# A global-filter and low-rank mixer kernel: stage-3 stores, group order and load lead rearranged

## The chip, the cores and the metric

The kernel runs on one core of a Trainium2 chip. The metric is the device time of one execution in microseconds (us). The profile is of one execution and has a span of 652.9 us.

## The reference

```python
def _attn_ref(x, filt_r, filt_i):            # x: 8 x 3136 x 256
    X = np.fft.rfft(x, axis=1)
    F = (filt_r + 1j * filt_i)[None, :, :]   # 1569 x 256
    return np.fft.irfft(X * F, n=x.shape[1], axis=1)

def _moe_ref(x, U, V, w_ch1, w_ch2):
    h = x.transpose(0, 2, 1) @ U @ V         # rank 32
    u = x + h.transpose(0, 2, 1)
    return u + np.maximum(u @ w_ch1, 0.0) @ w_ch2
```

The second function is applied to the result of the first. All inputs and outputs are float32; the kernel works in float16 with float32 accumulation.

## The kernel before

A sequence of 3136 positions is read as 64 x 49, and the Fourier transform over it is done as matmuls with small constant matrices. The eight batches are worked on in five units: two of one batch, then three of two batches (`UNITS`, L20). Each unit passes through four stages.

*Stage 1* (`f1`, L260) transforms the 64-long axis. It loads x on the GpSimd queue with a cast to f16, multiplies by `wf1` (L275 for unit 0, L284 for the others), copies the result from PSUM to the tile `asb` and stores it to the scratch tensor `ct1` in DRAM. In unit 0 the copies alternate between DVE (L279) and ACT (L277), and the stores between the sync queue and ACT's queue (L298). The position r=48 is a small separate piece (`al`, L313).

*Stages 2 and 3* (`mid`, L329) run over 33 frequencies k1 in the order of `KORDER`. For each, the tile `a2` read back from `ct1` (L324) is multiplied by `tf2` (L371, L376), DVE multiplies the result by the filter `fab` into `uv` (L379, L386), and two matmuls with `g3` (L342) give the inverse transform of that k1. ACT copies it into `esb` (L352), and it is stored to the scratch tensor `ct2`, two k1 at a time (L357), with single stores for the slots 0 and 31 (L354). The pool has three `esb` buffers of two k1 each. Unit 0 stores on the sync queue and the other units on the GpSimd queue. The second half of `fab` is a copy of the first with its two parts exchanged; only units 1 to 4 read it, and two SBUF-to-SBUF transfers make it (`mirror_filters`, L187 and L188).

*Stage 4 and the mixer* work on groups of tokens (`Group`, L434). `load_e2` (L406) reads `ct2` back as `e2` tiles and a small tile `e2l` for r=48. `low_rank` (L419) multiplies by the transformed U into `h1`. `stage4` (L443) makes the last transform and adds the V part, giving the mixer's input `ut`. `mm1` (L479) does one of eight chunks of 128 hidden channels with ReLU on ACT, and `mm2_part` (L502) does the second product of the previous group, adds the residual through an identity matmul (L499), copies to `och` (L537) and stores to the output (L492). A group has 512 tokens, except one per unit for r=48 with 64 tokens per batch, which comes last in its unit.

The order of the work is written out by hand (L541 to L613). Unit 0 passes through stages 1 to 3 alone. Then a loop over all groups with eight steps each runs `mm1` of the current group, `mm2_part` of the one before and, at t == 2, `stage4` of the next. A list `plan` says at which step a piece of stage 1 (`deal_f1`) or one k1 of stages 2 and 3 (`deal`) of a later unit goes in. The last pieces of `mid` end some steps before the unit's first group; `load_e2` follows at the step `mid_end`, and `low_rank` at nine steps ahead of the unit's first group. A step of the r=48 group counts as a full step here, although it has 64 or 128 columns instead of 512. The tile framework assigns buffers and semaphores and settles the instruction order of each engine from this program.

A tiny DVE copy into a tile (`hold`, L161) delays the transfer into that tile until its source has landed. In this way the loads of unit 0 are spread: `second_loads` (filters from the second part on, the rest of `tf2` and `g3`) wait for the first `a2`, `third_loads` (U, V, w1, w2) for a product in the middle of stage 2, and `fourth_loads` (x of unit 1) for `e2l`.

Of the kernel before, what the change touches and what calls it, by code (L numbers as in the profile page):

```python
# [102 lines left out]
def kernel(  # L103
# [92 lines left out]
    w2sb = cst.tile([128, 8 * DM], F16)  # L196

    def second_loads(src):
        for i in range(1, 4):
            hold(fab[0:1, 0, PARTS[i], 0:1], src)  # L200
            load_filters(PARTS[i], PARTS[i + 1])
        ka = PARTS[1] * 147
        hold(tf2[0:1, ka:ka + 1], src)
        nc.sync.dma_start(tf2[:, ka:], tf2_d[:, ka:])
        hold(g3[0:1, 2 * KA:2 * KA + 1], src)
        nc.sync.dma_start(g3[:, 2 * KA:], g_d[:, 2 * KA:])

    def third_loads(src):
        hold(usb[0:1, 0:1], src)
        nc.gpsimd.dma_start(usb, moe_U.rearrange("(q r) p -> q (r p)", q=NQ))  # L210
        nc.gpsimd.dma_start(vnat[0:32, :], moe_V)
        nc.gpsimd.dma_start(w1sb, moe_w_ch1.rearrange("(h dd) c -> dd h c", h=2))
        nc.gpsimd.dma_start(w2sb, moe_w_ch2.rearrange("(t cc) e -> cc t e", t=8))
# [46 lines left out]
    def f1(u, load_ahead=2):  # L260
# [4 lines left out]
        for c in range(nx):  # L265
# [47 lines left out]
        nc.scalar.copy(al, pf[0:m, 0, 0:DM])  # L313
# [16 lines left out]
    def mid(u, tag="z"):  # L330
# [4 lines left out]
        eng = nc.sync if u.n == 0 else nc.gpsimd  # L335

        def do_i1(k, uv):
# [14 lines left out]
            nc.scalar.copy(st["esb"][:, i, :], pe[0:98, 0:bd])  # L352
# [42 lines left out]
        while uvs:  # L395
            do_i1(*uvs.pop(0))
# [44 lines left out]
    groups = [Group(u, g) for u in units for g in range(u.ng + 1)]  # L441
# [37 lines left out]
    def mm1(gr, t):  # L479
        n = gr.ntok  # L480
        ph = ps.tile([128, 512], F32, tag="m", bufs=2, name="phh")
        for dh in range(2):
            nc.tensor.matmul(ph[:, 0:n], w1sb[:, dh * 1024 + t * 128:dh * 1024 + (t + 1) * 128],  # L483
                             gr.ut[:, dh, 0:n], start=(dh == 0), stop=(dh == 1))
# [58 lines left out]
    first = [sum(v.ng + 1 for v in units[:u.n]) * 8 for u in units]  # L543
# [22 lines left out]
    plan = [[] for _ in range(8 * len(groups) + 8)]  # L566

    def deal(gen, count, a, z):
        for i in range(count):
            assert a < z  # L570
            plan[a + i * (z - a) // count].append(gen)

    def deal_f1(u, a, at):

        k = a
        for _ in range(6 * u.nb + 1):
            while k % 8 not in at:
# [4 lines left out]
    for i in range(7):  # L582
        plan[(4, 5, 6, 7, 8, 9, 11)[i]].append(f1s[1])
    mid_end = [0, 42] + [first[u.n] - (21 if u.n == 2 else 25) for u in units[2:]]
    deal(mids[1], 34, 15, 41)
    deal_f1(units[2], 12, (0, 4, 6, 7))
    deal(mids[2], 34, 44, first[2] - 22)
    for u in units[3:]:
        deal_f1(u, first[u.n - 1] - 36, (4, 7))
        deal(mids[u.n], 34, first[u.n - 1] + 24, first[u.n] - 26)  # L590

    for n, gr in enumerate(groups):
        u = gr.u
        for t in range(8):
            mm1(gr, t)
            if t == 2 and n + 1 < len(groups):
# [3 lines left out]
            step = 8 * n + t  # L600
            for gen in plan[step]:
                next(gen)
            for v in units[2:]:
                if plan[step + 5].count(f1s[v.n]) and not v.x:
                    load_x(v, 0)
                    load_x(v, 1)
            if u.n + 1 < n_units:
# [36 lines left out]
```

## Time and profile before

| | |
|---|---|
| median of 3 runs | 656.44 us (655.64 to 658.65) |
| span of the profile | 652.9 us |
| PE busy | 573.9 us, 88% |
| DVE, ACT, POOL busy | 320.3, 334.2, 132.1 us |
| mean granted PE clock | 0.937 |
| DMA moved | 98.29 MB, mean 151 GB/s |
| first `mm1` matmul | 82.3 us |

Busy shares over the whole span mix a start-up in which units 0 and 1 are fed from DRAM, and a long part in which the mixer's matmuls run densely. The table by stretch, the chain of waits and the list of who waited for whom are therefore read for each stretch by itself. A unit boundary is where the first group of a new unit follows the last of the one before; these lie near 185, 275, 412 and 544 us.

### The profile page before, as it was taken

How to read it: one execution, taken by the hardware profiler on the slowest of the kernel's cores; microseconds unless marked ns; L12 is line 12 of the kernel's file. 1: busy time of each engine (PE TensorE's matmuls, PEld its weight loads, DVE VectorE, ACT ScalarE, POOL GpSimd, SP SyncE). 2: the span in 40 equal slices, each digit the busy share in tenths (PEclk: the TensorE clock that was granted, in tenths of full speed). 3: DMA queues.
4: the chain of work that ended last, by engine and by line, in shares of the span. 5: the costliest groups of instructions: out<-in, count | busy, mean ns of one | idle time of the engine just before them, and what ended most of it. 6: DMA issues, size and time to landing. Idle time of an engine off the chain costs nothing.

```text
span 652.9 us, 10703 instructions
## 1 busy us (share of the span) xinstructions
PE 573.9 (88%) x4161; PEld 383.9 (59%) x4161; DVE 320.3 (49%) x369; ACT 334.2 (51%) x625; POOL 132.1 (20%) x204
## 2 busy tenths in 40 slices
PE   3459249989879999699999999899999998999995
PEld 0347125656635666457666666576666775777774
DVE  2346114676567764135777752347777523333331
ACT  2213026655436666165666655555656654555553
POOL 4220604365431242030111231011111100000000
PEclk9955579998889999789999999999999999999999
DMA  9896687897994289964635289545261493033033
GB/s 170 228 213 143 141 168 154 194 223 194 203 307 122 75 183 237 282 115 104 178 97 166 48 221 283 143 111 163 85 190 41 124 210 104 3 98 82 16 98 104
DMA packets 44289, 98.29 MB, mean 151 GB/s; under 512 B 8194, under 2 KB 19104, under 8 KB 44042
## 3 DMA queue, kind: packets, MB, share of 16 engines
q1 hardware_dynamic: 25470, 57.98, 31.9%
q0 software_dynamic: 16800, 38.45, 27.3%
q10 hardware_dynamic: 1968, 1.17, 0.6%
q8 instruction: 32, 0.52, 0.3%
q14 instruction: 19, 0.16, 0.1%
HBM read 59.88 MB, written 51.38 MB: 170 GB/s over the span
## 4 chain that ended last, share of the span: by engine, by line
PE 62%; DMA 20%; issue 7%; POOL 4%; ACT 3%; SPq 3%; DVE 1%; ACTq 0%; POOLq 0%; DVEq 0%
PE phh L483 20%; PE pc L527 19%; PE pe L342 7%; DMA x<-in_x_dram 5%; PE pz L371 4%; DMA ct_0<-esb 3%; PE pu L468 3%; PE pc L499 3%; PE pu L474 3%; DMA e_2517<-ct_2 2%; DMA ct_1<-esb 2%; SPq L411 2%; PE pf L284 2%; DMA e_4187<-ct_3 1%; DMA ct_0<-asb 1%
## 5 line engine op out<-in xcount | busy, mean ns | idle before, releaser
L483 PE MATMUL phh<-ut,w1sb 128*128 128x512 f16 (+2 forms) x848 | 245.9, 370 | 3.9 <-DVE ut L477 2.6
L386 DVE TENSOR_TENSOR uv<-pz,fab 98x1024 f16<-98x1024 f32 (+1 forms) x132 | 141.8, 1087 | 53.8 <-PE pz L371 53.5
L352 ACT CAST esb<-pe 98x512 f16<-98x512 f32 (+1 forms) x160 | 79.5, 501 | 108.5 <-PE pe L342 69.0
L537 DVE COPY och<-pc 128x512 f32<-128x512 f32 x96 | 66.3, 690 | 104.8 <-PE pc L499 101.1
L483 PEld LDWEIGHTS <-w1sb 128*128 128x128 f16 x848 | 79.4, 100 | 43.8 <-issue 12.8
L477 DVE CAST ut<-pu 128x1024 f16<-128x1024 f32 x48 | 58.8, 1224 | 82.4 <-PE pu L474 82.1
L342 PE MATMUL pe<-uv,g_80 98*98 98x512 f16 (+1 forms) x330 | 91.3, 365 | 4.6 <-ACT esb L352 4.5
L342 PEld LDWEIGHTS <-g_80 98*98 98x98 f16 x330 | 45.6, 140 | 23.7 <-issue 10.9
L499 PE MATMUL pc<-idn,ut 128*128 128x128 f16 (+1 forms) x394 | 55.6, 222 | 0.0
L499 PEld LDWEIGHTS <-ut 128*128 128x128 f16 (+1 forms) x394 | 38.7, 99 | 6.5 <-issue 1.4
L284 PE MATMUL pf<-x,wf_64 128*128 128x512 f16 x84 | 27.0, 395 | 14.0 <-DMA x<-in_x_dram 11.2
L289 DVE CAST asb<-pf 128x1024 f16<-128x1024 f32 x21 | 25.7, 1223 | 25.7 <-PE pf L284 21.2
L156 POOL DMA_DIRECT2D x<-in_x_dram x48 | 26.2, 560 | 55.3 <-PE pf L284 25.2
L371 PEld LDWEIGHTS <-tf_77 98*98 98x98 f16 x165 | 23.0, 139 | 19.5 <-issue 16.3
L379 DVE TENSOR_TENSOR uv<-pz,fab 98x512 f16<-98x512 f32 x33 | 22.6, 691 | 15.6 <-PE pz L376 11.4
L357 POOL DMA_DIRECT2D ct_4<-esb x15 | 10.7, 712 | 72.2 <-ACT esb L352 65.8
L357 POOL DMA_DIRECT2D ct_3<-esb x15 | 10.7, 716 | 69.2 <-ACT esb L352 69.2
L287 ACT CAST asb<-pf 128x1024 f16<-128x1024 f32 x21 | 21.3, 1012 | 6.5 <-PE pf L284 4.8
L357 POOL DMA_DIRECT2D ct_2<-esb x15 | 11.0, 736 | 49.9 <-ACT esb L352 40.6
L284 PEld LDWEIGHTS <-wf_64 128*128 128x128 f16 x84 | 8.1, 100 | 21.5 <-DMA x<-in_x_dram 12.2
L424 PEld LDWEIGHTS <-ut_96 128*32 128x32 f16 x120 | 3.2, 101 | 24.7 <-DMA e_553<-ct_0 8.7
L357 POOL DMA_DIRECT2D ct_1<-esb x15 | 11.2, 746 | 20.8 <-ACT esb L352 20.7
(1483 smaller groups left out, 1152.5 us busy)
## 6 DMA issues: line engine op xcount, KB each, us to landing
out_dram<-och SPq DMA_DIRECT2D x96, 192.0 KB
x<-in_x_dram POOLq DMA_DIRECT2D x48, 256.0 KB, 7.8
out_dram<-och SPq DMA_DIRECT2D x16, 384.0 KB
ct_2<-asb POOLq DMA_DIRECT2D x12, 256.0 KB, 6.6
ct_3<-asb POOLq DMA_DIRECT2D x12, 256.0 KB, 5.9
ct_4<-asb POOLq DMA_DIRECT2D x12, 256.0 KB, 5.7
ct_2<-esb POOLq DMA_DIRECT2D x15, 196.0 KB, 4.1
ct_3<-esb POOLq DMA_DIRECT2D x15, 196.0 KB, 3.2
```

Source lines behind the costliest of these rows:

```text
L156: nc.gpsimd.dma_start(t[64 * p:64 * p + 64], dram(x.tensor, (u.b[0] * SEQ + 8 * c) * DM + st * p, [[NR * DM, 64], [1, 8 * DM]]))
L284: nc.tensor.matmul(pf[:, i, :], wf1, u.x[c][:, r:r + 2, :], start=True, stop=True)
L342: nc.tensor.matmul(pe[0:98, 0:bd], g3[:, (2 * k + l) * 98:(2 * k + l + 1) * 98], uv[:, l * bd:(l + 1) * bd], start=(k != 32 and l == 0), s ...
L352: nc.scalar.copy(st["esb"][:, i, :], pe[0:98, 0:bd])
L357: eng.dma_start(dram(u.ct2, (slot - 1) * 98 * bd, [[bd, 98], [98 * bd, 2], [1, bd]]), st["esb"])
L371: nc.tensor.matmul(pz[0:98, 0:bd], wz, a2[c][:, i, :], start=True, stop=True)
L386: nc.vector.tensor_mul(uv.rearrange("p (f b d) -> p f b d", f=2, b=nb), zin, fin)
L477: nc.vector.tensor_copy(gr.ut, pu)
L483: nc.tensor.matmul(ph[:, 0:n], w1sb[:, dh * 1024 + t * 128:dh * 1024 + (t + 1) * 128], gr.ut[:, dh, 0:n], start=(dh == 0), stop=(dh == 1))
L499: nc.tensor.matmul(o[:, dh * 128:dh * 128 + 128], gr.ut[:, dh, t0:t0 + n], idn, start=False, stop=(dh == 1), skip_group_check=True)
L527: nc.tensor.matmul(o, gr.h[tt][:, i * 128:(i + 1) * 128], w2sb[:, tt * DM:(tt + 1) * DM], start=(tt == 0), stop=False, skip_group_check=True)
L537: nc.vector.tensor_copy(dst, gr.pc.rearrange("p (b j d) -> p b j d", b=u.nb, j=u.jc))
```

## The change

- Stage-3 stores (`do_i1`): for one-batch units, four k1 go into one `esb` buffer and one store; for two-batch units still two. All units store on the sync queue. The last full k1 of the order and the k1 pair 0 and 32 keep stores of their own.
- Group order: the r=48 group of every unit but the last moves from the end of the unit to the place behind its third group.
- Lead: times in `plan` are counted in full steps (the r=48 group counts by its columns); stages 2 and 3 of units 1 and 2 end earlier, and `load_e2` and `low_rank` follow at steps counted from the unit's start. `stage4` moves from t == 2 to t == 4.
- Start-up: unit 0's stage-1 copies all go to DVE, the second filter part is loaded when stage 1 ends, x of unit 1 is requested as soon as the second `e2` tile has landed, and the mirror copies wait for `h1`.
- w2 is loaded with 8 KB contiguous for each partition instead of eight rows of 1 KB; the hidden channels are numbered accordingly, and `mm1` takes its 128 columns of w1 with a step of eight elements.
- The name of the change speaks of filler matmuls: neither version issues any.

```diff
+    w1v = w1sb.rearrange("p (h cc t) -> p h cc t", h=2, t=8)
+    def load_part(i, src):
+        hold(fab[0:1, 0, PARTS[i], 0:1], src)
+        load_filters(PARTS[i], PARTS[i + 1])
     def second_loads(src):
-        for i in range(1, 4):
-            hold(fab[0:1, 0, PARTS[i], 0:1], src)
-            load_filters(PARTS[i], PARTS[i + 1])
+        for i in range(2, 4):
+            load_part(i, src)
...
-        nc.gpsimd.dma_start(w2sb, moe_w_ch2.rearrange("(t cc) e -> cc t e", t=8))
+        nc.gpsimd.dma_start(w2sb, moe_w_ch2.rearrange("(cc t) e -> cc (t e)", t=8))
...
-                        if i:
-                            nc.scalar.copy(dst[:, i, :], pf)
-                        else:
-                            nc.vector.tensor_copy(dst[:, i, :], pf)
+                        nc.vector.tensor_copy(dst[:, i, :], pf)
...
-        nc.scalar.copy(al, pf[0:m, 0, 0:DM])
+        if u.n == 0:
+            nc.vector.tensor_copy(al, pf[0:m, 0, 0:DM])
+            load_part(1, al[0:1, 0:1])
+        else:
+            nc.scalar.copy(al, pf[0:m, 0, 0:DM])
...
-        eng = nc.sync if u.n == 0 else nc.gpsimd
+        ne = 4 // nb
...
-            slot = 0 if k == 32 else k
-            if slot % 2 == 1:
-                st["esb"] = sb.tile([98, 2, bd], F16, tag="esb", bufs=3, name="esb")
-            i = 1 - slot % 2
+            pos = 31 if k == 32 else k - 1
+            i = pos % ne
+            if i == 0:
+                st["esb"] = sb.tile([98, ne, bd], F16, tag="esb", bufs=3, name="esb")
             nc.scalar.copy(st["esb"][:, i, :], pe[0:98, 0:bd])
-            if slot in (0, 31):
-                eng.dma_start(dram(u.ct2, slot * 98 * bd, [[bd, 98], [1, bd]]),
-                                    st["esb"][:, i, :])
-            elif i:
-                eng.dma_start(
-                    dram(u.ct2, (slot - 1) * 98 * bd, [[bd, 98], [98 * bd, 2], [1, bd]]),
+            if pos in (30, 31):
+                nc.sync.dma_start(
+                    dram(u.ct2, (0 if pos == 31 else 31 - i) * 98 * bd,
+                         [[bd, 98], [98 * bd, 1 if pos == 31 else i + 1], [1, bd]]),
+                    st["esb"][:, i if pos == 31 else 0:i + 1, :])
+            elif i == ne - 1:
+                nc.sync.dma_start(
+                    dram(u.ct2, (k - i) * 98 * bd, [[bd, 98], [98 * bd, ne], [1, bd]]),
                     st["esb"])
...
-    groups = [Group(u, g) for u in units for g in range(u.ng + 1)]
+    groups = []
+    for u in units:
+        g = list(range(u.ng))
+        g.insert(3 if u.n + 1 < len(units) else u.ng, u.ng)
+        groups += [Group(u, i) for i in g]
...
-            nc.tensor.matmul(ph[:, 0:n], w1sb[:, dh * 1024 + t * 128:dh * 1024 + (t + 1) * 128],
+            nc.tensor.matmul(ph[:, 0:n], w1v[:, dh, :, t],
                              gr.ut[:, dh, 0:n], start=(dh == 0), stop=(dh == 1))
...
-    first = [sum(v.ng + 1 for v in units[:u.n]) * 8 for u in units]
+    when, starts = [], []
+    now = 0.0
+    for n, gr in enumerate(groups):
+        if n == 0 or gr.u is not groups[n - 1].u:
+            starts.append(now)
+        for _ in range(8):
+            when.append(now)
+            now += gr.ntok / 512
+    def step_at(w):
+        return next(i for i, v in enumerate(when) if v >= w)
...
     load_e2(units[0])
-    hold(fab[0:1, 1, 0, 0:1], units[0].e2l[0:1, 0:1])
-    hold(fab[64:65, 1, 0, 0:1], units[0].e2l[0:1, 0:1])
+    fourth_loads(units[0].e2[1][0:1, 0, 0, 0:1])
+    low_rank(units[0])
+    hold(fab[0:1, 1, 0, 0:1], units[0].h1[0:1, 0:1])
+    hold(fab[64:65, 1, 0, 0:1], units[0].h1[64:65, 0:1])
     mirror_filters(0, NK)
-    fourth_loads(units[0].e2l[0:1, 0:1])
-    low_rank(units[0])
     stage4(groups[0])
...
-    for i in range(7):
-        plan[(4, 5, 6, 7, 8, 9, 11)[i]].append(f1s[1])
-    mid_end = [0, 42] + [first[u.n] - (21 if u.n == 2 else 25) for u in units[2:]]
-    deal(mids[1], 34, 15, 41)
-    deal_f1(units[2], 12, (0, 4, 6, 7))
-    deal(mids[2], 34, 44, first[2] - 22)
+    deal(f1s[1], 7, 4, 11)
+    deal(mids[1], 34, 17, 34)
+    deal_f1(units[2], 12, (0, 2, 6, 7))
+    deal(mids[2], 34, 44, S[2] - 25)
+    load_step = {step_at(35): units[1], step_at(S[2] - 24): units[2]}
     for u in units[3:]:
-        deal_f1(u, first[u.n - 1] - 36, (4, 7))
-        deal(mids[u.n], 34, first[u.n - 1] + 24, first[u.n] - 26)
+        deal_f1(u, S[u.n - 1] - (38 if u.n == 3 else 48), (1, 7))
+        deal(mids[u.n], 34, S[u.n - 1] + (21 if u.n == 3 else 12), S[u.n] - 26)
+        load_step[step_at(S[u.n] - 25)] = u
+    rank_step = {step_at(S[u.n] - 6): u for u in units[1:]}
...
-            if t == 2 and n + 1 < len(groups):
+            step = 8 * n + t
+            if step in rank_step:
+                low_rank(rank_step[step])
+            if t == 4 and n + 1 < len(groups):
                 stage4(groups[n + 1])
...
-                if step == mid_end[u.n + 1]:
-                    load_e2(units[u.n + 1])
-                if step == first[u.n + 1] - 9:
-                    low_rank(units[u.n + 1])
+            if step in load_step:
+                load_e2(load_step[step])
```

`S[n]` is the start of unit n in full steps: 0, 49, 98, 196 and 294.

More of the change, by code (lines that the diff above doesn't have):

```diff
@@ L395, in mid @@
         while uvs:
-            do_i1(*uvs.pop(0))
+            last = uvs.pop(0)
+            do_i1(*last)
         yield
@@ L557 @@
     load_e2(units[0])
-    hold(fab[0:1, 1, 0, 0:1], units[0].e2l[0:1, 0:1])
-    hold(fab[64:65, 1, 0, 0:1], units[0].e2l[0:1, 0:1])
+    fourth_loads(units[0].e2[1][0:1, 0, 0, 0:1])
+    low_rank(units[0])
+    hold(fab[0:1, 1, 0, 0:1], units[0].h1[0:1, 0:1])
+    hold(fab[64:65, 1, 0, 0:1], units[0].h1[64:65, 0:1])
     mirror_filters(0, NK)
-    fourth_loads(units[0].e2l[0:1, 0:1])
-    low_rank(units[0])
     stage4(groups[0])
     plan = [[] for _ in range(8 * len(groups) + 8)]
+    S = starts
     def deal(gen, count, a, z):
         for i in range(count):
-            assert a < z
-            plan[a + i * (z - a) // count].append(gen)
+            plan[step_at(a + i * (z - a) / count)].append(gen)
     def deal_f1(u, a, at):
-        k = a
+        k = step_at(a)
         for _ in range(6 * u.nb + 1):
-            while k % 8 not in at:
+            while k % 8 not in at or groups[k // 8].last:
                 k += 1
@@ L580, in deal_f1 @@
             k += 1
-    for i in range(7):
-        plan[(4, 5, 6, 7, 8, 9, 11)[i]].append(f1s[1])
-    mid_end = [0, 42] + [first[u.n] - (21 if u.n == 2 else 25) for u in units[2:]]
-    deal(mids[1], 34, 15, 41)
-    deal_f1(units[2], 12, (0, 4, 6, 7))
-    deal(mids[2], 34, 44, first[2] - 22)
-    for u in units[3:]:
-        deal_f1(u, first[u.n - 1] - 36, (4, 7))
-        deal(mids[u.n], 34, first[u.n - 1] + 24, first[u.n] - 26)
+    deal(f1s[1], 7, 4, 11)
[3 more added lines that the diff above has]
+    load_step = {step_at(35): units[1], step_at(S[2] - 24): units[2]}
+    for u in units[3:]:
+        deal_f1(u, S[u.n - 1] - (38 if u.n == 3 else 48), (1, 7))
+        deal(mids[u.n], 34, S[u.n - 1] + (21 if u.n == 3 else 12), S[u.n] - 26)
+        load_step[step_at(S[u.n] - 25)] = u
+    rank_step = {step_at(S[u.n] - 6): u for u in units[1:]}
+    x_step = {max(0, next(i for i, p in enumerate(plan) if f1s[u.n] in p) - 5): u for u in units[2:]}
     for n, gr in enumerate(groups):
@@ L599 @@
                 mm2_part(groups[n - 1], t)
-            step = 8 * n + t
             for gen in plan[step]:
                 next(gen)
[L603 to L607, printed above, removed]
-                if step == mid_end[u.n + 1]:
-                    load_e2(units[u.n + 1])
-                if step == first[u.n + 1] - 9:
-                    low_rank(units[u.n + 1])
+            if step in x_step:
+                load_x(x_step[step], 0)
+                load_x(x_step[step], 1)
+            if step in load_step:
+                load_e2(load_step[step])
     for t in range(8):
```

## The prediction

> **What bounds the kernel now.** I first asked in which stretches TensorE (PE) is not busy, because the page gives PE 88% of the span. The table by stretch, whose columns are the stretch, its length, the busy time of PE, of the weight loads, of VectorE (DVE), ScalarE (ACT) and GpSimd (POOL), the granted PE clock, the DMA share and GB/s, answers it:
> ```profile
> 26.00:66.00 40.00, 30.54 (x137) 25.16 (x135) 23.22 (x37) 11.96 (x35) 10.04 (x16) 0.62 0.87 185
> 66.00:82.00 16.00, 3.73 (x35) 1.95 (x36) 2.33 (x10) 0.37 (x1) 10.03 (x13) 0.50 0.65 145
> 82.00:100.00 18.00, 9.60 (x34) 4.19 (x34) 2.65 (x3) 4.67 (x8) 1.00 (x2) 0.69 0.77 157
> 145.00:190.00 45.00, 36.95 (x251) 24.50 (x249) 26.19 (x33) 18.71 (x45) 19.99 (x32) 0.89 0.88 221
> 255.00:290.00 35.00, 28.23 (x205) 17.04 (x204) 9.03 (x11) 13.65 (x27) 6.57 (x11) 0.85 0.84 216
> 290.00:400.00 110.00, 110.00 (x814) 74.01 (x812) 70.33 (x69) 68.08 (x119) 20.36 (x31) 1.00 0.56 148
> 400.00:420.00 20.00, 16.80 (x153) 11.01 (x152) 6.18 (x7) 9.17 (x20) 2.73 (x4) 1.00 0.77 218
> 535.00:555.00 20.00, 17.60 (x160) 11.88 (x159) 5.75 (x7) 9.37 (x20) 0.00 (x0) 1.00 0.42 111
> 555.00:645.00 90.00, 90.00 (x757) 65.85 (x756) 27.09 (x33) 52.21 (x92) 0.00 (x0) 1.00 0.20 54
> ```
> From 290 us on PE is full except at two unit boundaries, so time can be won only from the start-up and the four boundaries. PE idle there is 9.5, 12.3, 8.4, 8.1, 6.8, 3.2 and 2.4 us in the seven rows below full; the clock of 0.69, 0.89 and 0.85 costs about 3, 4 and 4 us more (busy time times the missing clock). The chain of waits in order of time names what each stretch waits for (start, length, what):
> ```profile
> 31.07 8.62 DMA ct_0<-esb
> 40.46 8.05 DMA ct_0<-esb
> 78.83 17.52 DMA x<-in_x_dram
> 168.05 8.07 DMA ct_1<-esb
> 176.91 7.00 DMA e_1552<-ct_1
> 258.06 15.12 DMA e_2517<-ct_2
> 395.31 9.38 DMA e_4187<-ct_3
> ```
> These are stage-3 stores, the unit-1 input, and the last-stage loads: the things the change touches. The table of who waited for whom adds, for the first unit:
> ```profile
> ACT esb L352 <- DMA ct_0<-esb: 16.7, 7, 4.2
> DVE uv L379 <- DMA fab<-in_filt_i_dram: 4.0, 1, 4.0
> ```
> Last, the weight loads, since the change spreads the columns of w1 (busy us, mean ns):
> ```profile
> L483 PEld LDWEIGHTS <-w1sb 128*128 128x128 f16 x848 | 79.4, 100 | 43.8 <-issue 12.8
> L342 PEld LDWEIGHTS <-g_80 98*98 98x98 f16 x330 | 45.6, 140 | 23.7 <-issue 10.9
> ```
>
> **What the Trainium skill says.** "TensorE: Matmul & The Clock Gate", section on weight-path perf modes: a load of 128 non-fp32 columns is taken the fast way, "packed or strided", up to a column step of 1,024 elements. The trace agrees on the first half: 128 columns take 100 ns, 98 columns 140 ns. No load here is strided. "SBUF — State Buffer", section Door 1: lines are 16 bytes, and an access that goes to a new line each time pays; a step of 8 f16 is exactly one line. The two pages pull apart, and the trace doesn't decide. "DMA: Bandwidth & Descriptors", section "Issuing engines are not separate DMA queues": moving a DMA to another issuer saves only issue time. The trace has that price: the same store line takes 0.71 us on POOL for units 1 to 4 and 0.31 us on the sync queue for unit 0. The TensorE page's part 1 says that the clock falls to half after an idle window of about 3.4 us; here it stood at 0.50 in 265 to 270 us, after 4.5 us without work.
>
> **The parts, one by one.**
>
> *Stage-1 evacuation of unit 0 on DVE, filter part 1 early.* 12 copies of 0.69 us on DVE begin at 7.6 us; with the input's pace they end near 17.5, against 19.3 on ACT now, whose copies sat 4.8 us behind its own DMA issues. The filter part (400 KB as moved, 2 us at 200 GB/s) then goes in front of the first stage-2 loads, which takes part of it back. I take 0.5 us won.
>
> *Stage 3 of unit 0.* 33 products at the 0.86 us pace seen before the first stall plus 2.4 us for the U-hat matmuls make 30.8 us; the products ran from 26.3 to 64.9, so 7.8 us were lost, 4.0 to the filter part and the rest to full esb buffers. Both causes go: 12 instead of 6 slices fit in the three buffers. But the bytes stay: 7.4 MB at 185 GB/s with the DMA engines full until 55 us. Only the 400 KB moved forward and the w2 load (13.6 us to landing in 1 KB rows, w1 9.9 us) shorten the queue. Bounds 2 and 7.8, I take 5.
>
> *Mirror of the filters behind the low-rank matmuls.* Now the two 808 KB copies start at 77.7 and 78.7 us, and the unit-1 input, issued at 78.3, lands at 96.4; alone such a load takes 6 to 8 us. The change issues the input first and holds the mirror until h1 (79.0 us). The first tile then lands near 85, before it is asked for near 88; the next two share with the mirror and may stall PE 1 to 3 us. Out of 8.1 us of wait and 3 us of low clock I take 7 (bounds 3 and 10).
>
> *Stage 3 of unit 1 earlier, stores off POOL.* Stage 3 ends at step 34 instead of 40, and the loads have 8 steps until they are used instead of 5: at 1.5 us a step 4.5 us more for a path of 16 us (168.0 last store, 183.9 landed). POOL loses 17 issues of 0.7 us per unit, so input loads no longer queue behind stores that wait for ACT (a 2.4 us PE stall at 147). Behind a store waiting on the sync queue now stand out-stores and stage-2 loads; their buffers are three deep, and I cost that at nothing. With the DMA engines at 0.88 of their time in the stretch, I take 5 of 12 (bounds 1 and 10).
>
> *Unit 2.* The e2 loads get 18 steps instead of 12 before the low-rank matmuls. From the last store (243.6) to the last landing (273.2) is 30 us; 19 steps of 1.3 us are 25 us, and the sync queue should save some. I take 6 of 10.8 (bounds 3 and 10).
>
> *Units 3 and 4.* At 540 us the chain goes low-rank, h1, ut (1.24 us), matmul with only the small r=48 group beside it. With that group moved inside and low-rank 6 steps ahead, full-size work covers it: 3 and 2.4 us, the idle of the two rows. The order of groups and stage 4 two steps later add no work.
>
> *What the earlier schedule costs.* Stage 3 of unit 1 runs at 2 slices a step. DVE then has 2 x 0.69 for uv, 0.33 for ut and och (1.22 + 2 x 0.69 over 8), 0.30 for the stage-1 copies of unit 2: 2.0 us a step. PE has 1.03 (a dense group is 90 us x 68/757 = 8.1 us, 8 steps), 0.64 for six 256-column matmuls at 0.107 and 0.21 for stage 1: 1.9 us. So DVE becomes the bound for 17 steps, and for unit 2 (1.17 slices of 1.22 us a step) both are near 1.9. I take 4 us lost, bounds 0 and 8.
>
> *Strided w1.* Each of 384 full steps loads w1 twice. In the dense part a load hides under the matmul before it: 0.107 us (256 columns) or 0.213 us (512). If the strided load still goes the fast way, the cost is 0. If it lasts 0.21 us, the first load of each step sticks out by 0.107: 384 x 0.107 = 41 us. I take 0, since the fast-load page names strides expressly, and keep 41 as a rival.
>
> **The sum.** 0.5 + 5 + 7 + 5 + 6 + 3 + 2.4 - 4 = 24.9 us won; 656.4 - 24.9 = 631.5, so **631 us**.
>
> **The rivals.**
> - *The DMA engines give it back.* Until 200 us they are 0.75 to 0.92 busy. If every earlier start only meets a full queue, the terms 5, 7 and 5 shrink to 3 together: 656.4 - (0.5 + 3 + 6 + 3 + 2.4 - 4) = about **646**. For it: saturation to 55 us and from 165 to 195. Against: 65 to 70, 90 to 105 and 125 to 135 are far from full.
> - *The weight loads of w1 become the bound*, slower than before: 631 + 41 = **672**. For it: one 16-byte line per column. Against: the fast-load rule, and PEld is busy only 66 of 90 us in the dense part.
> - *Every wait goes*: the upper bounds, 0.5 + 7.8 + 10 + 10 + 10 + 3 + 2.4 - 4 = 39.7, **617**. Against: the first 60 us move the same bytes.
> - *It cancels*: DVE as the bound costs 8 and the boundaries keep their waits, **656**. Against: the lead at unit 2 grows by half.
>
> **Chances.** Forecast 0.60, DMA rival 0.16, strided loads 0.16, all waits gone 0.04, even 0.04. Faster by over 0.5% is the sum 0.80, slower 0.16, the same 0.04. The range 614 to 655 holds the forecast with its bounds, the DMA rival and most of the low case, and leaves the strided case outside.
>
> **What the profile after would show.** Right: no DMA x in the chain near 80 to 96 us; ACT's wait for ct_0 stores well under 16.7 us; first mm1 near 77 instead of 82; clock 1.00 at unit 2's boundary; the L483 weight loads still near 100 ns. Wrong: L483 loads at 150 ns or more with PE slower than 8.1 us a group after the last boundary; or DVE near 100% between 105 and 140 us with PE waiting for uv; or sync-queue stores that wait so long that e2 lands no earlier before its use than now.

## The result and the profile after

| | before | after |
|---|---|---|
| median | 656.04 us (653.43 to 658.65, 4 runs) | 631.90 us (631.14 to 634.63, 4 runs) |
| ratio | 1 | 0.964 (95% interval 0.9591 to 0.9688) |
| span of the profile | 652.9 us | 630.4 us |
| mean granted PE clock | 0.937 | 0.960 |
| PE, POOL busy | 573.9, 132.1 us | 567.5, 83.2 us |

The change wins 24 us, 3.6%. The prediction was 631 us, from a sum of 24.9 us. The total is right; the parts are not all right, as the table of progress further down shows. The higher mean clock is not where the time comes from: the fastest of the four runs of the changed kernel (631.14 us) had 0.936. Executions over 1.5% above the fastest of their kernel are left out of the figures below (one of a7, one of b2, four of the kernel before).

The table by stretch of the changed kernel, with the columns explained in the prediction (stretch, length, busy time of PE, weight loads, DVE, ACT and POOL, granted clock, DMA share, GB/s):

```profile
26.00:66.00 40.00, 30.26 (x137) 24.52 (x137) 23.53 (x41) 12.16 (x34) 10.11 (x14) 0.68 0.81 188
66.00:82.00 16.00, 3.80 (x36) 1.97 (x36) 1.81 (x10) 0.74 (x2) 8.91 (x13) 0.50 0.76 158
82.00:100.00 18.00, 17.18 (x88) 9.84 (x88) 6.22 (x6) 10.57 (x18) 3.52 (x6) 0.82 0.83 192
100.00:145.00 45.00, 39.83 (x286) 26.96 (x285) 29.30 (x40) 25.33 (x55) 16.44 (x27) 1.00 0.97 232
145.00:190.00 45.00, 40.27 (x297) 27.87 (x296) 27.82 (x31) 24.78 (x49) 7.21 (x13) 1.00 0.86 212
255.00:290.00 35.00, 32.21 (x268) 23.49 (x266) 14.36 (x16) 18.11 (x34) 6.12 (x10) 1.00 0.65 155
400.00:420.00 20.00, 20.00 (x156) 14.80 (x155) 11.56 (x12) 12.25 (x22) 0.00 (x0) 1.00 0.54 155
535.00:555.00 20.00, 20.00 (x163) 15.33 (x162) 5.91 (x7) 11.60 (x21) 0.00 (x0) 1.00 0.23 59
```

The first two rows are as empty as before: the start-up up to 82 us was not shortened. The third row went from 9.60 to 17.18 us of PE work. The boundary rows filled up, two of them wholly, and their clock rose from 0.89 and 0.85 to 1.00. The row from 100 to 145 us is a loss: 39.83 us of PE work, with the DMA engines at 0.97, where the kernel before had 43.61:

```profile
100.00:145.00 45.00, 43.61 (x301) 27.92 (x299) 27.34 (x35) 28.51 (x53) 21.38 (x33) 1.00 0.83 190
```

The DMA transfers in the chain of waits of the changed kernel (start, length, what):

```profile
12.76 7.67 DMA tf_77<-tf
20.49 6.04 DMA ct_0<-al
26.60 2.61 DMA a_168<-ct_0
32.22 7.86 DMA a_217<-ct_0
42.96 12.22 DMA a_342<-ct_0
...
109.64 8.58 DMA a_848<-ct_1
136.26 13.15 DMA ct_1<-esb
157.59 5.75 DMA ct_1<-esb
164.13 5.68 DMA e_1469<-ct_1
237.52 18.64 DMA e_2424<-ct_2
279.31 5.19 DMA a_3057<-ct_3
```

The 17.5 us input transfer at 78.8 us is gone. In its place, between 105 and 165 us, stand stage-2 loads and stage-3 stores of unit 1. That both e2 loads are still in the chain means little without the waits. The low-rank matmuls waited for them before:

```profile
PE ph L424 <- DMA e_1552<-ct_1: 3.1, 1, 3.1
PE ph L424 <- DMA e_2511<-ct_2: 4.4, 1, 4.4
```

They hardly wait now:

```profile
PE ph L433 <- DMA e_1469<-ct_1: 0.3, 1, 0.3
PE ph L433 <- DMA e_2424<-ct_2: 0.2, 1, 0.2
```

The store at 20.49 us is slower than before, when it took 2.69 us. In unit 0 the store links of the chain from 31 us on have given way to two stage-2 loads.

From the list of what the DMA issues of the sync queue waited for in the changed kernel (us in total, times, longest):

```profile
SPq L365 <- ACT esb L358: 129.8, 51, 6.6
```

From PE's own waits between 100 and 200 us, and the weight-load row of the page:

```profile
PE pz L379 <- DMA a_846<-ct_1: 3.0, 1, 3.0
```
```profile
L497 PEld LDWEIGHTS <-w1sb 128*128 128x128 f16 x848 | 105.9, 145 | 31.6 <-issue 8.9
```

The stores' 129.8 us of waiting are on the sync queue now, and what stood behind them there did not suffer by it, as the low-rank waits above show. PE now has a wait for the first stage-2 load of unit 1 (3.0 us), where the longest such wait for unit 1 was 0.2 us before; that load is issued at 109.2 us, ahead of the first stage-3 store of unit 1 (120.7 us), so it did not stand behind one. ACT's wait for its unit-0 `esb` buffers fell from 16.7 us to 2.7 us. The weight loads of w1, now strided, take 145 ns instead of 100.

**Where the time was won.** Take the start of the second `och` copy of a 512-token group as a milestone. Such groups are counted from 0; group 6 is the first of unit 1, 12 of unit 2, 24 of unit 3, 36 of unit 4, and 47 is the last. Times in us, from the traces (the labels are those of the experiments below):

| group | before | after | gain | b1 | b2 | b3 | a3 | a7 |
|---|---|---|---|---|---|---|---|---|
| 0 | 111.5 | 100.8 | 10.7 | 100.4 | 102.4 | 100.1 | 109.0 | 100.7 |
| 3 | 157.9 | 156.5 | 1.4 | 156.2 | 155.9 | 147.9 | 157.4 | 158.4 |
| 6 | 213.6 | 201.6 | 12.0 | 212.2 | 212.3 | 202.9 | 212.7 | 212.0 |
| 12 | 294.4 | 276.1 | 18.3 | 293.1 | 293.3 | 285.8 | 286.3 | 284.5 |
| 24 | 429.6 | 410.0 | 19.6 | 430.9 | 428.6 | 421.2 | 419.2 | 422.1 |
| 36 | 558.4 | 535.1 | 23.3 | 559.7 | 557.4 | 550.0 | 544.4 | 548.2 |
| 47 | 645.4 | 622.6 | 22.8 | 646.6 | 644.3 | 637.0 | 631.8 | 635.7 |

The row of group 3 is the surprise. 10.7 us are won at group 0, all but 1.4 are gone at group 3, and 12.0 are there again at group 6. Most of this is no loss: the milestone has not the same work before it in both kernels. The r=48 group of unit 0 now lies ahead of group 3, and more of the stage-2 products of unit 1 (33 instead of 25). The stretches from group 0 to 3 and from 3 to 6 before:

```profile
111.51:157.87 46.36, 42.55 (x289) 28.02 (x287) 30.47 (x42) 27.16 (x55) 21.62 (x33) 0.96 0.84 211
157.87:213.60 55.73, 49.31 (x338) 30.65 (x337) 37.35 (x39) 28.25 (x61) 19.37 (x31) 0.94 0.78 206
```

and after:

```profile
100.76:156.53 55.77, 50.03 (x360) 34.37 (x359) 37.37 (x52) 32.65 (x73) 20.61 (x34) 1.00 0.97 233
156.53:201.58 45.05, 40.74 (x284) 26.69 (x283) 29.69 (x29) 23.67 (x43) 2.88 (x6) 1.00 0.75 195
```

Up to group 3 PE does 360 matmuls instead of 289 and is busy 7.5 us longer; its idle time rises by only 1.9 us, from 3.8 to 5.7, although the DMA engines are 0.97 busy instead of 0.84. From group 3 to 6 the work that was moved forward is missing. Over both stretches together PE is idle 10.0 us after and 10.2 before. The rows of kernels with different group orders are therefore best compared at group 6 and later.

### The profile page after: what moved, and what is told of

The parts are those of the page before. It is cut to its first block, busy times and chain, and to the rows that moved or that the text cites. A ratio compares the mean times of both kernels' runs of the same rounds, so it can differ in the third digit from the quotient of the medians.

```text
span 630.4 us, 10659 instructions
## 1 busy us (share of the span) xinstructions
PE 567.5 (90%) x4161; PEld 404.9 (64%) x4161; DVE 323.1 (51%) x376; ACT 332.1 (53%) x618; POOL 83.2 (13%) x136
## 4 chain that ended last, share of the span: by engine, by line
PE 76%; DMA 18%; ACT 2%; SPq 1%; issue 1%; DVE 1%; POOL 0%; ACTq 0%; POOLq 0%
PE phh L497 24%; PE pc L541 23%; PE pe L347 8%; PE pz L379 5%; PE pu L482 3%; PE pu L488 3%; PE pc L513 3%; DMA ct_1<-esb 3%; DMA e_2424<-ct_2 3%; PE pf L285 2%; DMA a_342<-ct_0 2%; SPq L420 1%; DMA a_848<-ct_1 1%; DMA a_217<-ct_0 1%; DMA e_540<-ct_0 1%; DMA tf_77<-tf 1%
## 5 line engine op out<-in xcount | busy, mean ns | idle before, releaser
L497 PEld LDWEIGHTS <-w1sb 128*128 128x128 f16 x848 | 105.9, 145 | 31.6 <-issue 8.9
L347 PEld LDWEIGHTS <-g_80 98*98 98x98 f16 x330 | 44.5, 138 | 18.3 <-issue 4.7
L513 PE MATMUL pc<-idn,ut 128*128 128x128 f16 x394 | 55.0, 219 | 0.0
L379 PEld LDWEIGHTS <-tf_77 98*98 98x98 f16 x165 | 22.6, 137 | 32.8 <-issue 21.5
L513 PEld LDWEIGHTS <-ut 128*128 128x128 f16 x394 | 38.5, 98 | 6.8 <-issue 0.8
L290 DVE CAST asb<-pf 128x1024 f16<-128x1024 f32 x21 | 25.6, 1221 | 19.6 <-PE pf L285 18.8
L387 DVE TENSOR_TENSOR uv<-pz,fab 98x512 f16<-98x512 f32 x33 | 22.6, 691 | 12.5 <-PE pz L384 12.1
L285 PE MATMUL pf<-x,wf_64 128*128 128x512 f16 x84 | 25.7, 379 | 0.1
L379 PE MATMUL pz<-a_168,tf_77 98*98 98x256 f16 x4 | 1.6, 406 | 14.7 <-DMA a_168<-ct_0 14.3
L305 POOL DMA_DIRECT2D ct_4<-asb x12 | 8.3, 700 | 36.2 <-ACT asb L288 36.2
L305 POOL DMA_DIRECT2D ct_2<-asb x12 | 8.5, 713 | 29.5 <-ACT esb L358 25.8
```

The source lines that it names most:

```text
L285: nc.tensor.matmul(pf[:, i, :], wf1, u.x[c][:, r:r + 2, :], start=True, stop=True)
L347: nc.tensor.matmul(pe[0:98, 0:bd], g3[:, (2 * k + l) * 98:(2 * k + l + 1) * 98], uv[:, l * bd:(l + 1) * bd], start=(k != 32 and l == 0), s ...
L379: nc.tensor.matmul(pz[0:98, 0:bd], wz, a2[c][:, i, :], start=True, stop=True)
L497: nc.tensor.matmul(ph[:, 0:n], w1v[:, dh, :, t], gr.ut[:, dh, 0:n], start=(dh == 0), stop=(dh == 1))
L513: nc.tensor.matmul(o[:, dh * 128:dh * 128 + 128], gr.ut[:, dh, t0:t0 + n], idn, start=False, stop=(dh == 1), skip_group_check=True)
```

## The experiments

The "a" kernels are the changed kernel with one part undone, the "b" kernels are the kernel before with parts added, "c" is the changed kernel with something new. Ratios are to the kernel before, measured beside it. Differences to the changed kernel are of medians from different sittings, in which the median of the kernel before lay between 656.0 and 657.3 us; of a difference under some 3 us nothing is concluded. Times inside a kernel are from one profiled execution each. In seven kernels that leave unit 0's start-up as in the changed kernel or nearly so (the change, a3, a4, a6, a7, a8, c1) the first product starts between 28.8 and 30.2 us, which gives the spread of such times.

**b1, the input request and the mirror alone.**

```diff
     load_e2(units[0])
-    hold(fab[0:1, 1, 0, 0:1], units[0].e2l[0:1, 0:1])
-    hold(fab[64:65, 1, 0, 0:1], units[0].e2l[0:1, 0:1])
+    fourth_loads(units[0].e2[1][0:1, 0, 0, 0:1])
+    low_rank(units[0])
+    hold(fab[0:1, 1, 0, 0:1], units[0].h1[0:1, 0:1])
+    hold(fab[64:65, 1, 0, 0:1], units[0].h1[64:65, 0:1])
     mirror_filters(0, NK)
-    fourth_loads(units[0].e2l[0:1, 0:1])
-    low_rank(units[0])
```

> The kernel before with one part of the change alone: the input of unit 1 is requested when the second e2 tile has landed, and the mirror copies wait for h1. Theory A (the mirror was what held the input back, and it is the largest single term): the 8.1 us wait for x at 88 to 96 us goes with its low clock, the first group ends some 9 to 11 us earlier, and the whole time falls to about 646 to 648 us. Theory B (the gain of the first group comes from the start-up as a whole, and an earlier input only meets full DMA queues): the time stays above 652 us.

Measured: 657.0 us against 657.3, ratio 0.9999 (0.9965 to 1.0034): no difference. Yet the wait itself went. The first stage-1 matmul of unit 1 starts at 86.9 us instead of 96.5, and group 0 is 11.1 us earlier. By group 6 only 1.4 us are left. Its chain of waits shows where they went:

```profile
129.94 11.51 DMA x<-in_x_dram
161.69 6.97 DMA ct<-esb
169.45 10.36 DMA e<-ct
```

These are the same three links as in the kernel before (`x` at 137.55, last store at 168.05, e2 at 176.91), 6 to 8 us earlier at most. Removing the first wait only lets the next ones be reached sooner; theory A had the wait right and its worth wrong.

**a3, the reverse: the changed kernel with the old order of mirror and input.** The edit is that of b1 backwards.

> The changed kernel with the mirror copies and the input of unit 1 in the old order: both wait for e2l, the mirror first. Theory A: the wait of 8 us for x comes back at about 88 us, the first group ends 9 to 11 us later, and since PE is full later on most of it stays: 639 to 643 us. Theory B (the later boundaries have slack that takes it up): below 636 us.

Measured: 642.42 us, ratio 0.9773 (0.9685 to 0.9860), 10.5 us above the changed kernel. The transfer is back, and the first stage-1 matmul of unit 1 is at 96.31 us:

```profile
78.85 17.33 DMA x<-in_x_dram
```

So the same edit is worth nothing alone and 10.5 us in company. At group 6 a3 stands at 212.7 us, only 0.9 us ahead of the kernel before: the new schedule and the new stores, without the early input, gain next to nothing up to there. Gains that do not add up in this way suggest pieces in series, which the next two kernels build up.

**b2, b1 plus unit 1's schedule.**

```diff
-        plan[(4, 5, 6, 7, 8, 9, 11)[i]].append(f1s[1])
-    mid_end = [0, 42] + ...
-    deal(mids[1], 34, 15, 41)
+        plan[4 + i].append(f1s[1])
+    mid_end = [0, 35] + ...
+    deal(mids[1], 34, 17, 34)
...
-                if step == first[u.n + 1] - 9:
+                if step == first[u.n + 1] - (13 if u.n == 0 else 9):
```

> The kernel before with two parts together: the mirror behind h1 (which alone gave nothing), and unit 1 given the changed kernel's schedule: stage 1 in steps 4 to 10, stages 2 and 3 in steps 17 to 33, the last-stage loads at step 35 and low-rank four steps sooner. Stores, buffers and group order are as before. Theory A (the early input and the early stage 3 of unit 1 are in series: each alone is taken up by the other's wait): the first group of unit 1 ends 8 us or more before the 213.6 us of the kernel before, and the time falls to 644 to 650 us. Theory B (the stage-3 stores with two one-batch k1 in each buffer hold unit 1 back, as the kernel with two k1 suggests): the gain at unit 1 is under 4 us, the time 653 us or more.

Measured: 654.81 us against 657.14, ratio 0.9966 (0.9943 to 0.9988). The first theory falls: two pieces are not enough, and group 6 is still at 212.3 us.

**b3, b2 plus the new stage-3 stores**, four k1 at a time for one-batch units (the last full ones, 29 to 31, go as three) and all on the sync queue (the hunk of `do_i1` in the change, nothing else).

> The kernel before with three parts together: mirror behind h1, the changed schedule of unit 1 (these two together gave 655 us), and now the stage-3 stores of the changed kernel, four one-batch k1 in a buffer and on the sync queue in every unit. The r=48 group stays last, units 2 to 4 keep their old schedule, the start-up its old copies and filter order. Theory A (the stores were the missing piece for unit 1): the first group of unit 1 ends at 206 us or earlier instead of 212.3, and the time falls to 645 to 650 us. Theory B (the place of the r=48 group, whose undoing alone cost 11 us, is needed as well): the first group of unit 1 ends after 209 us and the time is 651 us or more.

Measured: 644.03 us against 656.22, ratio 0.9800 (0.9754 to 0.9845). Group 6 is at 202.9 us, 1.3 us from the changed kernel. The stores were the third piece. (The stores alone, without the other two, were not run; a3 is the nearest to it.) What they do shows on the order of work on POOL. In b2, where the stores wait there for ACT, unit 2's input loads stand behind them (start, length, engine, line, what, and the idle time before):

```profile
131.41 0.73 POOL L357 DMA_DIRECT2D ct<-esb  x1 [1.51 <-ACT esb L352]
132.13 1.12 POOL L156 DMA_DIRECT2D x<-in_x_dram  x2
...
143.96 0.72 POOL L357 DMA_DIRECT2D ct<-esb  x1 [6.14 <-ACT esb L352]
144.68 0.57 POOL L144 DMA_DIRECT2D xl<-in_x_dram  x1
```

In b3 the same loads:

```profile
121.83 1.11 POOL L156 DMA_DIRECT2D x<-in_x_dram  x2
...
125.80 0.57 POOL L144 DMA_DIRECT2D xl<-in_x_dram  x1
```

The `xl` load leaves 19 us earlier. Between 125 and 160 us b2 has these two waits, and b3 has neither:

```profile
DVE asb L289 <- DMA ct<-asb: 5.4, 1, 5.4
...
PE pf L284 <- DMA x<-in_x_dram: 4.7, 2, 4.5
```

The two are one stall: PE stands from 137.1 to 141.6 us for an input of unit 2 that came late, and DVE's wait ends at 142.7 us, with the end of the matmuls that PE then does. The granted clock in b2 falls to 0.73 from 135 to 145 us, where b3 has 1.00. b3 passes group 3 at 147.9 us, 8 us before b2, of which 2.3 us were there at group 0, and from 105 to 165 us its DMA engines are 0.93 busy instead of 0.82. The Trainium skill, "DMA: Bandwidth & Descriptors", says in its section on issuing engines that another issuer saves only issue time. Costing the move by that alone would miss what it did here: it also freed what stood in the queue behind a waiting store. b3 does not separate the move from the size of the stores; a4 and a6 look at the two from the other side.

**a4, the stores of units 1 to 4 on the GpSimd queue again**, their size as in the change. The edit of the `dma_start` shown is made at both stores.

```diff
         ne = 4 // nb
+        eng = nc.sync if u.n == 0 else nc.gpsimd
...
-                nc.sync.dma_start(
+                eng.dma_start(
```

> The changed kernel with the stage-3 stores of units 1 to 4 on the GpSimd queue, still four k1 (unit 1) or two at a time. Theory A (the queue saves only issue time; what gains is the lead): GpSimd is busy some 35 us more, input loads of unit 2 wait behind stores again, and the time rises by 0 to 4 us, 631 to 636 us. Theory B (the sync queue is what shortens the way from the last store to the last-stage loads): the stall at the boundaries to units 1 and 2 comes back, above 638 us.

Measured: 636.34 us, ratio 0.9678 (0.9602 to 0.9754). That is 4.4 us above the changed kernel by the medians; the two intervals overlap, and the value lies between the ranges of the two theories. Its profile is of the slowest of its four runs (638.61 us). There group 6 is 6.7 us later, and an input load is back in the chain:

```profile
133.60 10.65 DMA x<-in_x_dram
```

**a6, two k1 in a store in every unit.**

```diff
-        ne = 4 // nb
+        ne = 2
```

> The changed kernel with two k1 for each store in every unit, so that units 0 and 1 have half the esb space and twice the stores. Theory A (bytes bound the start-up, not the buffers: unit 0's stage 3 ended at 64.9 us in both kernels although the waits for esb went from 16.7 to a few us): the last product of unit 0 stays within 2 us, and the time within 2 us of 631.9. Theory B (the buffers matter, and the gain was eaten by the later start): the last product comes 4 us or more later, and the time rises by 2 us or more.

Measured: 643.15 us (637.96 to 647.20), ratio 0.9778 (0.9684 to 0.9873), 11 us slower than the changed kernel. In unit 0, where I had looked for the gain, the last product ends only 1.0 us later (66.4 against 65.4). The loss is in unit 1: ACT waits for full `esb` buffers again, five times and 9.7 us in all between 105 and 165 us, against 2.0 us in the changed kernel, and group 6 is at 208.8 us. This line of its list covers the whole span, units 0 and 1 together:

```profile
ACT esb L358 <- DMA ct<-esb: 24.0, 10, 4.3
```

So four k1 in a store seem to pay as buffer depth, twelve slices in place of six, in a stretch where a store takes up to 13 us to land. a6 halves the depth and doubles the number of stores together, so the waits for full buffers point to the depth, but the two are not separated.

**a7, the r=48 group at the end of its unit again.**

```diff
-        g.insert(3 if u.n + 1 < len(units) else u.ng, u.ng)
+        g.insert(u.ng, u.ng)
```

> The changed kernel with the r=48 group at the end of every unit, with the starts counted in the same way and low-rank six full steps ahead of the next unit. Theory A (full-size work beside the chain of low-rank, h1 and ut is what the inner place buys): the boundaries to units 3 and 4 lose 0 to 2 us each, since low-rank is still five full steps ahead; 632 to 637 us. Theory B (the place of the group means nothing once low-rank comes early): within 1 us of 631.9.

Measured: 641.87 us (640.07 to 644.76, three runs), ratio 0.9769 (0.9683 to 0.9855), 10.0 us slower than the changed kernel and more than either theory said. In the profile (of the run of 644.76 us) group 6 is 10.4 us late already, before any boundary of units 2 to 4. Low-rank matmuls of unit 1 have no DMA wait there. Between 105 and 165 us its list of waits has this instead:

```profile
ACT esb L358 <- DMA ct<-esb: 6.2, 1, 6.2
PE pz L379 <- ACT esb L358: 6.1, 1, 6.1
```

One store (138.60 to 154.86 us in its chain) holds the last `esb` buffer for 6.2 us, ACT stands, and PE, which needs ACT to empty a PSUM tile, stands with it. The granted clock falls too, to 0.78 from 145 to 160 us; from group 0 to group 6 it is 0.95, where the changed kernel has 1.00. Unit 1's last store is issued at 164.8 us instead of 157.6. Why the place of the group makes just this store late is not settled: the framework orders each engine's instructions anew, and the transfers meet in another order.

**a1, the second filter part back among the second loads.**

```diff
-        for i in range(2, 4):
+        for i in range(1, 4):
             load_part(i, src)
...
-            load_part(1, al[0:1, 0:1])
```

> The changed kernel with the second filter part loaded with the others again, after the first a2 tile has landed. Theory A (the early filter part holds back the stores and read-back before the first product, which came 3.7 us later than before the change): the first product starts near 26 us instead of 29.3, but stage 2 then waits about 4 us for that filter part at its tenth k1, so that the first mm1 stays within 1.5 us and the time within 2 us of 631.9. Theory B (the 3.7 us come from putting all copies on DVE): the first product stays at 29 us, and the wait for the filter is added, about 635 us. Theory C (the early part costs 3.7 us and gains nothing): about 628 us.

Measured: 634.05 us, ratio 0.9637 (0.9563 to 0.9711), no difference from the change. The first product starts at 26.75 us instead of 30.01, the `al` store takes 3.52 us instead of 6.04, and the old wait is back:

```profile
19.50 3.52 DMA ct<-al
23.09 2.86 DMA a<-ct
27.46 9.37 DMA fab<-in_filt_i_dram
```

So the early load removes one wait and lengthens another. The first `mm1` is at 80.7 us here, 2 us before the changed kernel, and nothing of that is left at the end.

**a5, unit 0's stage-1 copies split between DVE and ACT again.**

```diff
-                        nc.vector.tensor_copy(dst[:, i, :], pf)
+                        if i:
+                            nc.scalar.copy(dst[:, i, :], pf)
+                        else:
+                            nc.vector.tensor_copy(dst[:, i, :], pf)
```

> The changed kernel with unit 0's stage-1 copies on DVE and ACT in turn, as before the change. Theory A (the start-up does not set the end): the first product moves by up to 3 us, the time stays within 2 us of 631.9. Theory B (DVE alone saves time at the start, because ACT's copies waited behind its own DMA issues): the first product comes 2 us or more later and the time rises to 634 us or more.

Measured: 632.14 us, ratio 0.9633 (0.9550 to 0.9715), no difference. The first product is at 28.0 us, 2 us earlier with the copies split; the other kernels with all copies on DVE and the early filter part lie between 28.8 and 30.2 us, so what the copies make of it may be under 1 us.

**a2, w1 and w2 in their old layout.**

```diff
-        nc.gpsimd.dma_start(w2sb, moe_w_ch2.rearrange("(cc t) e -> cc (t e)", t=8))
+        nc.gpsimd.dma_start(w2sb, moe_w_ch2.rearrange("(t cc) e -> cc t e", t=8))
...
-            nc.tensor.matmul(ph[:, 0:n], w1v[:, dh, :, t],
+            nc.tensor.matmul(ph[:, 0:n], w1sb[:, dh * 1024 + t * 128:dh * 1024 + (t + 1) * 128],
```

> The changed kernel with w1 read in contiguous columns and w2 loaded in rows of 1 KB, as before the change. Theory A (a strided load takes 145 ns instead of 100 but lies under the matmul before it): the loads return to 100 ns, the dense groups keep 8.3 us, and the time changes by less than 2 us, 630 to 635 us, with w2 landing later. Theory B (the strided loads cost something in each step): the time falls by 3 us or more, below 629 us.

Measured: 635.75 us, ratio 0.9666 (0.9595 to 0.9738), not faster. The weight loads are short again:

```profile
L497 PEld LDWEIGHTS <-w1sb 128*128 128x128 f16 x848 | 77.4, 99 | 40.4 <-issue 11.6
```

A dense group after the last boundary takes 8.21 us here and 8.25 us in the changed kernel, so nearly all of the 46 ns of each strided load is hidden. Its median is 3.9 us above that of the changed kernel although group 0 comes 2.6 us earlier in the profile; the loss comes up to group 6, and its cause is not settled.

**a8, a3 with each mirror transfer cut in two.** A transfer over 49 partitions goes as 48 and 1.

```diff
-        nc.sync.dma_start(fab[0:NR, 1, a:z, :], fab[NR:98, 0, a:z, :])
-        nc.sync.dma_start(fab[NR:98, 1, a:z, :], fab[0:NR, 0, a:z, :])
+        for lo, hi in ((0, 48), (48, NR)):
+            nc.sync.dma_start(fab[lo:hi, 1, a:z, :], fab[NR + lo:NR + hi, 0, a:z, :])
+            nc.sync.dma_start(fab[NR + lo:NR + hi, 1, a:z, :], fab[lo:hi, 0, a:z, :])
```

> The changed kernel with the mirror ahead of the input again (642 us), but each mirror copy of 49 partitions cut into one of 48 and one of 1. Theory A (a copy over 49 partitions runs on few DMA engines, and the input waits on just those): with 48 the mirror is through in half the time, x comes 4 us or more sooner than at 96.3 us, and the time falls by 2 to 8 us, 634 to 640 us. Theory B (the copies are slow for their bytes, or x waits its turn in any case): x still comes after 94 us and the time stays at 640 to 644 us.

Measured: 638.94 us, ratio 0.9728 (0.9686 to 0.9770), 3.5 us faster than a3 by the medians. The input lands 3.7 us earlier (92.5 us instead of 96.2), and the first stage-1 matmul of unit 1 starts at 92.62 us instead of 96.31:

```profile
79.14 13.34 DMA x<-in_x_dram
```

The price of the collision thus depends on the form of the transfer it collides with, and not on its bytes alone. From 88 to 92 us, with the input still out, the DMA engines are 0.70 busy in a3 and 1.01 in a8. That fits theory A, but the profile does not say which engines carried which transfer, so it stays a theory.

**c1, an attempt at a better kernel**: the changed kernel with the mirror cut as in a8, and stages 2 and 3 of unit 3 three steps later, since its first `a2` was waited for at 279 us.

```diff
-        deal(mids[u.n], 34, S[u.n - 1] + (21 if u.n == 3 else 12), S[u.n] - 26)
+        deal(mids[u.n], 34, S[u.n - 1] + (24 if u.n == 3 else 12), S[u.n] - 26)
```

> A try at a better version: the changed kernel with the mirror cut into 48 and 1 partitions, and with stages 2 and 3 of unit 3 starting three steps later (24 instead of 21 steps into unit 2), since PE waited 2.1 us at 280 us for the first read-back of that unit. If both waits are real and nothing else binds: 1 to 4 us less than 631.9, so 628 to 631 us. If the DMA queues hand the wait on: 631 to 634 us.

Measured: 634.59 us (631.86 to 639.69), ratio 0.9658 (0.9616 to 0.9699): no gain, and the two edits are not separated. The wait at 279 us left the chain, but group 6 is 4.6 us later; the profile is of the slowest of the six runs (639.69 us). Nothing that was tried beats the changed kernel.

## Why the prediction was right, and where it was not

**The total** was 0.9 us off, but by luck: two errors of 6 and 4 us cancel in it, the start-up and the mirror. The rivals' 617, 646, 656 and 672 us all lie outside the runs.

**Start-up, predicted 0.5 + 5, measured -0.5.** The first `mm1` is at 82.78 us instead of 82.26, not near 77. The step that failed is the early filter part, "which takes part of it back": it took all of it back and more. Issued at 16.8 us, the load stretches the `al` store to 6.04 us, which took 2.69 us before and 3.52 us in a1, and the first product starts 3.7 us later than before (30.0 us against 26.3). The copies themselves ended at 15.9 us, sooner than the 17.5 I had summed, and this gained nothing: the `al` store left at 20.49 us, right behind the landing of the first part of `tf2`, where it had left at 19.96. Stage 3 of unit 0 itself kept to its bounds of 2 and 7.8 us. "Both causes go" was true, with ACT's wait down from 16.7 to 2.7 us, and the products ran in 35.4 us instead of 38.6. But that is 3.2 us won against 3.7 lost. In place of ACT's waits PE now waits 4.6 us in all for three later stage-2 loads of unit 0 (`a_257`, `a_302`, `a_342`), with the DMA share at 1.01 from 30 to 55 us, and w2 took 12.5 us to land, hardly less than its 13.6. That the bytes set the end of this stage is still only argued: in a1, a2, a5 and a6 the first product started between 26.8 and 29.7 us, and the last ended between 63.4 and 66.4. a1 shows moreover that 2 us won at 82 us do not reach the end.

**Mirror behind the low-rank matmuls, predicted 7 of at most 10.** From the first `mm1` to group 0 the gain is 10.7 + 0.5 = 11.2 us; the mirror's own share is 8.2 us by undoing it (a3 against the change at group 0) and 11.1 us by adding it (b1 against before). The mechanism was right, the term too small, with the total above its upper bound of 10: PE went from 9.60 to 17.18 us of work in the row to 100 us and hardly stalled on the two tiles that I had put at 1 to 3 us.

**Unit 1, predicted 5 - 4 = 1, measured 12.0 - 10.7 = 1.3.** The difference is right; neither term was measured alone, and the reason for the 4 is wrong. I had named DVE. Between 105 and 140 us DVE is busy 23.1 of 35 us and mostly waits for PE, and PE waits for stage-2 loads (3.0 and 1.1 us) with the DMA engines at 0.98. The rival "the DMA engines give it back" names the right resource for these waits, but they are small: from group 0 to group 3 PE is idle 1.9 us more than before, and from group 3 to group 6 it is idle 2.1 us less (4.3 against 6.4).

**Unit 2, predicted 6, measured 6.3; units 3 and 4, predicted 5.4, measured 1.3 + 3.7 = 5.0 up to group 36.** These held, by the steps given: the wait for `e_2511` fell from 4.4 to 0.2 us, and PE has no idle time in either row of units 3 and 4. No experiment undoes these parts by themselves. b3, which lacks these parts among others, loses 8.4 us against the change from group 6 to 12 and 5.2 from there to 36.

**Strided w1, predicted 0.** It nearly held, though the loads are longer. Beside a 256-column matmul of 107 ns a load of 145 ns could have stuck out by 38 ns, 0.3 us in a group of eight steps. From group 36 to 46 ten groups took 82.12 us in each of the five profiles with packed columns (before, a2, b1, b2, b3) and 82.48 us in each of the nine with strided ones. So the cost is there, 0.04 us a group; if it were the same in all 48 groups, an estimate from these figures, it would be 1.7 us in all. The page "TensorE: Matmul & The Clock Gate" leads near the right choice, but a strided load is not as short as a packed one, so neither of the two cases I had set out (100 ns, or 210 ns and 41 us) is what happened.

**What the sum hid.** The parts are no independent terms. Undone one at a time (a1 to a7) they cost 2.2, 3.9, 10.5, 4.4, 0.2, 11.3 and 10.0 us by the medians, 42 us together, while the whole change is worth 24; by the ratios the sum is about 30 us. The three large ones alone (a3, a6, a7) make 32 us by the medians and 26 by the ratios. Added one after the other, the first gives 0.3 us, which is nothing beyond the noise, two give 2.3, three 12.2. Up to unit 1's first group the early input, the early stage 3 and the deep stores off POOL stand in series: an early input alone only reaches the next wait sooner, and undoing the mirror's place or the stores brings a wait back. That is shown by b1, b2 and b3, and by a3, a4 and a6; the early stage 3 was never undone alone. That the place of the r=48 group is a fourth link of the same kind is only argued, since a7's late store has no cause that the trace names.

## What to carry to other kernels

A wait in the chain, with the low clock that follows it, is about the most that its removal gives, and the rest of the chain up to the next full resource decides how much of it stays; sum such terms only across stretches that PE already fills, as at the boundaries of units 2 to 4 here. Where waits stand in series, test a part by adding it alone and by undoing it alone: here the same edit gave nothing the one way and 10.5 us the other. When the order of the work changes, count what lies before a milestone before a difference there is called a loss. Before moving a load forward, look for the short transfer that it will run beside, and before moving a stage forward, at the DMA share of the stretch it moves into.

## What the hardware showed that I had not expected

- A load of 128 weight columns that lie eight f16 apart took 145 ns, and 99 to 100 ns packed. With 512 tokens in a group this cost 0.04 us of 8.2 us a group.
- Two SBUF-to-SBUF transfers of 808 KB over 49 partitions each held an input load of 256 KB a transfer for 17.3 us (a3); cut into 48 partitions and one, for 13.3 us (a8).
- A 400 KB filter load with a cast, put ahead of one short store on another queue, stretched that store: 2.7 us before and 3.5 us in a1 without it, 5.4 to 7.2 us in the changed kernel, a3, a4, a6, a7, a8 and c1 with it.
- In the full stretch of unit 1 a store of 196 KB in the chain took 13.2 us to land, and 16.3 us in a7; stores of half the size in a6 took 6.5 to 10.5 us there.
